# Spectral filter and gated FFN on one Trainium2 core: seven-product down projection, 64x64 tiles, a shorter inverse transform and a list-scheduled order

## The chip, the core and the metric

The kernel runs on one core of one Trainium2 chip. The metric is the device time of one execution in microseconds (us); the profile's span, from the first to the last instruction of the program, is a little shorter than that time. TensorE (PE) multiplies matrices and writes PSUM, which has eight banks of 128 partitions x 512 float32 columns. VectorE (DVE) and ScalarE (ACT) empty PSUM; GpSimd (POOL) and SyncE (SP) here mostly issue transfers. Each engine works through its own queue in order and waits on semaphores.

## The reference

```python
def _A_ref(x, w_r, w_i):                    # x [1, 2048, 512]
    X = rfft2(x.astype(float32))            # over positions (2048) and features (512)
    X = X * (w_r + 1j * w_i)                # w [2048, 257]
    return irfft2(X, s=(2048, 512)).astype(bfloat16)
def _B_ref(x, w_gate, w_up, w_down):        # 512 -> 1792 -> 512
    h = gelu(x @ w_gate) * (x @ w_up)
    return h @ w_down
xn = layernorm(A_x)
out = A_x + _A_ref(xn, w_r, w_i) + _B_ref(xn, w_gate, w_up, w_down)
```

All inputs are bfloat16. `B_x` is not used.

## The kernel before, in words

The 2048 positions are cut into 16 tiles `j` of 128 positions and four blocks `b` of four tiles. Two streams of work share all engines.

The FFN stream. A block is normalised (`ln_stat`, `ln_aggr`, `ln_norm`), transposed on PE (`trans`, L373) and kept as `xnT`. For each of 14 slices `fc` of the 1792 hidden columns, `gate` (L585) and `up` (L600) each make one bank of 128 hidden columns x 512 positions from four matmuls of 512 columns. ScalarE takes the gelu of the gate bank (L588, into `gl`), VectorE multiplies the up bank by it (L606, into `hT`). `down` (L642) makes one bank of 128 positions x 512 features from 14 matmuls of 512 columns, in three parts; VectorE adds the bank to `x_sb` (L657). The down tiles of block `b` stand among the gate and up units of block `b+1`. The last tile is done in two halves of 256 columns (`last_down`, L622, added at L627).

The spectral stream. The feature transform is unit D (`butter` on VectorE, L395 to L399, then four matmuls, L413 to L416). The 2048-point transform over positions is split into 64 x 32: unit A does the 64-point part (L437, L441), with the two halves of a tile on the two halves of PE's rows; the result goes through DRAM (`scr1`) to be laid out anew as `tv`. Unit B does the 32-point part of step `h` (16 steps): four matmuls with 64 output rows each, two of which stand side by side in PE's columns. ScalarE copies the result to `xc` (L468), VectorE multiplies by the filter in four instructions (`m1`, `m2`, then their difference and sum into `yy`, L474 to L477), unit C does the inverse 32-point part (L488), ScalarE copies it to `vp` (L494), and it goes through DRAM (`scr2`) to `vv`. Unit E (L522) does the inverse 64-point part of a tile, four matmuls of 128 columns; ScalarE writes `zt` (L529), and GpSimd puts one row of it in place (L530). Unit F (L548 to L551) does the inverse feature transform with four matmuls of 256 columns, one pair for even and one for odd frequencies. ScalarE copies the bank to `eo` (L556), VectorE adds and subtracts the halves (L561, L562) and adds the result to `x_sb` (L565).

```python
                for ri in range(2):                          # unit_B
                    for hh in range(2):
                        ins = e.matmul(bank(bk + ri)[64 * hh:64 * hh + 64, 0:257], be[:, 64 * ri:64 * ri + 64], tv[:, 16 * hh + h, :],
...
                for ri in range(2):                          # unit_C
                    for hh in range(2):
                        ins = e.matmul(bank(bk + hh)[:, 0:257], cm[64 * hh:64 * hh + 64, h, ri, :], y[64 * hh:64 * hh + 64, ri, 0:KD],
...
                    for fc in range(f0, f1):                 # down
                        ins = e.matmul(bank(bk), hT[b % 2][:, fc, jj * P:(jj + 1) * P], wd_sb[:, fc, :], start=(fc == 0), stop=(fc == NFC - 1))
```

The order is written by hand. The main loop runs over blocks and slices; after each gate, each up and each part of a down, `hook` runs what a table (`plan`, filled by `at`) sets down for that point: the statistics, transposes, units D, A, B, C, E, F and the late loads. `take` chooses PSUM banks by a running estimate of when each comes free. SyncE issues nearly all transfers (L304), in the order of the program; GpSimd issues the late loads (`load_late`, L308), each behind the last matmul put ahead of it in the order: the down weights, the constants `be`, `cm`, `gm`, and the filter `Wr`, `Wi` in 16 loads of 128.5 KB. `_Prog.op` derives the semaphore waits from the keys that each operation reads and writes.

Of the kernel before, what the change touches and what calls it, by code (L numbers as in the profile page):

```python
# [13 lines left out]
S = 2048  # L14
D = 512
# [13 lines left out]
def _constants():  # L29

    tp = 2.0 * np.pi
    q = np.arange(64)
    l32 = np.arange(32)
    k1 = np.arange(64)

    dd = np.arange(P)[:, None]
    m64 = np.arange(64)[None, :]
    a0 = tp * dd * (4 * m64) / D  # L40
    a2 = tp * dd * (4 * m64 + 2) / D
    im0 = -np.sin(a0)
    im0[:, 0] = np.cos(np.pi * np.arange(P))
    FE0 = np.concatenate([np.cos(a0), im0], 1)
    FE2 = np.concatenate([np.cos(a2), -np.sin(a2)], 1)
    FO = []
    for c in range(2):
        d = dd + P * c
        kodd = np.stack([4 * m64[0] + 1, 4 * m64[0] + 3]).reshape(1, 128)
        a = tp * d * kodd / D  # L50
        FO.append(np.concatenate([np.cos(a), -np.sin(a)], 1))
    FD = np.concatenate([FE0, FE2, FO[0], FO[1]], 1)

    AM = np.zeros((P, NJ, 2, P))
    for b in range(2):
        for j in range(NJ):
            l = 16 * b + j
            th = tp * (np.outer(q, k1) / 64.0 + l * k1[None, :] / S)
            c, s = np.cos(th), np.sin(th)
            AM[64 * b:64 * b + 64, j, 0, :] = np.concatenate([c, -s], 1)  # L60
            AM[64 * b:64 * b + 64, j, 1, :] = np.concatenate([s, c], 1)

    BM = np.zeros((32, 2, 2, 2, 32, 2))
    th = tp * np.outer(l32, l32) / 32.0
    for kl in range(2):
        BM[:, 0, kl, 0, :, kl] = np.cos(th)
        BM[:, 1, kl, 0, :, kl] = np.sin(th)
        BM[:, 0, kl, 1, :, kl] = -np.sin(th)
        BM[:, 1, kl, 1, :, kl] = np.cos(th)
    BM = BM.reshape(2, 16, 4, P).transpose(0, 2, 1, 3).reshape(P, P)  # L70

    CM = np.zeros((2, 32, 2, 16, 2, 2, 2, 32))
    for hh in range(2):
        for kl in range(2):
            for h in range(16):
                kk = 32 * kl + 16 * hh + h
                th = tp * (np.outer(l32, l32) / 32.0 + kk * l32[None, :] / S)
                CM[hh, :, kl, h, 0, 0, kl, :] = np.cos(th)
                CM[hh, :, kl, h, 0, 1, kl, :] = np.sin(th)
                CM[hh, :, kl, h, 1, 0, kl, :] = -np.sin(th)  # L80
                CM[hh, :, kl, h, 1, 1, kl, :] = np.cos(th)
    CM = CM.reshape(P, 16, 2, P)

    EM = np.zeros((2, 16, 2, 2, 2, 64))
    for hh in range(2):
        for kl in range(2):
            kk = 32 * kl + 16 * hh + np.arange(16)
            th = tp * np.outer(kk, q) / 64.0
            EM[hh, :, 0, kl, 0, :] = np.cos(th)
            EM[hh, :, 0, kl, 1, :] = np.sin(th)  # L90
            EM[hh, :, 1, kl, 0, :] = -np.sin(th)
            EM[hh, :, 1, kl, 1, :] = np.cos(th)
    EM = EM.reshape(2, 16, 4, P).transpose(0, 2, 1, 3).reshape(P, P)

    d2 = np.arange(256)[None, :]
    G = np.zeros((P, 4, 256))
    for c in range(2):
        kd = (2 * np.arange(P) + c)[:, None]
        a = tp * kd * d2 / D
        G[:, 2 * c, :] = 2.0 * np.cos(a)  # L100
        G[:, 2 * c + 1, :] = -2.0 * np.sin(a)
    G[0, 0, :] = 1.0
    G[0, 1, :] = np.cos(np.pi * np.arange(256))
    ID = np.eye(P)
    f16 = lambda a: np.ascontiguousarray(a.astype(np.float16))
    return (f16(ID), f16(FD), f16(AM.reshape(P, -1)), f16(np.concatenate([BM, EM], 1)),
            f16(CM.reshape(P, -1)), f16(G.reshape(P, -1)))


class _Prog:  # L110
# [17 lines left out]
    def op(self, eng, fn, r=(), w=(), dma=False, after=()):  # L128
        deps = [(ev, True) for ev in after]
        for k in r:  # L130
            if k in self.writer:
                deps.append((self.writer[k], True))
        for k in w:
            if k in self.writer:
                deps.append((self.writer[k], False))
            for ev in self.readers.get(k, ()):
                deps.append((ev, False))
        need = {}
        for (st, val), raw in deps:
            if st == eng and not dma and (eng == "pe" or not raw):  # L140
                continue
            need[st] = max(need.get(st, 0), val)
# [9 lines left out]

# [39 lines left out]

def bass_parallel_sum__spectral_gfnet__glu_gated_geglu__prompt_kernel(
# [22 lines left out]
    wgv = B_w_gate.rearrange("(dc p) f -> p dc f", p=P)  # L216
    wuv = B_w_up.rearrange("(dc p) f -> p dc f", p=P)
    wdv = B_w_down.rearrange("(fc p) d -> p fc d", p=P)

    with ExitStack() as es:  # L220
# [3 lines left out]
        pr = _Prog(nc, es)  # L224
        op = pr.op
# [3 lines left out]
        xnT = sb("xnT", [P, 4, S], F16)  # L229

        arena = sb("arena", [P, 9216], F16)
        am = arena[:, 0:4096].rearrange("p (j r c) -> p j r c", j=NJ, r=2)
        fold = [arena[:, 4096 + 2048 * i:6144 + 2048 * i].rearrange("p (a c) -> p a c", a=4) for i in range(2)]
        ev1 = arena[:, 8192:9216].rearrange("p (a c) -> p a c", a=2)
        vv = arena[:].bitcast(BF16)[:, 0:32 * KD].rearrange("p (l c) -> p l c", l=32)
        AKEYS = ["am", "ev1"] + [("fold", i, a) for i in range(2) for a in range(4)]
        wg_sb = sb("wg", [P, 4, FF], BF16)
        wu_sb = sb("wu", [P, 4, FF], BF16)
        wd_sb = sb("wd", [P, NFC, D], BF16)
        hT = [sb("hT%d" % i, [P, NFC, 512], BF16) for i in range(2)]  # L240
        ident = sb("ident", [P, P], F16)
        fd = sb("fd", [P, 768], F16)
        be = sb("be", [P, 2 * P], F16)
        cm = sb("cm", [P, 16, 2, P], F16)
        gm = sb("gm", [P, 4, 256], F16)
        Wr = sb("Wr", [P, 16, 258], BF16)
        Wi = sb("Wi", [P, 16, 258], BF16)
        xs = [sb("xs%d" % i, [P, D], F16) for i in range(4)]
        tt = [sb("tt%d" % i, [P, 2, KD], F16) for i in range(4)]
        tv = sb("tv", [P, 32, KD], F16)  # L250
        xc = [sb("xc%d" % i, [P, 2, 258], F16) for i in range(2)]
        m1 = [sb("m1_%d" % i, [P, 2, 258], BF16) for i in range(2)]
        m2 = [sb("m2_%d" % i, [P, 2, 258], BF16) for i in range(2)]
        yy = [sb("yy%d" % i, [P, 2, 258], BF16) for i in range(4)]
        vp = [sb("vp%d" % i, [P, 2, KD], BF16) for i in range(4)]
        NZ = 4
        zt = [sb("zt%d" % i, [P, 4, P], BF16) for i in range(NZ)]
        row = sb("row", [32, 64], BF16)
        z256 = xn[:].rearrange("p a d -> p (a d)").bitcast(BF16)
        gl = [sb("gl%d" % i, [P, 512], BF16) for i in range(3)]  # L260
        eo = [sb("eo%d" % i, [P, 512], BF16) for i in range(2)]
        ys2 = [sb("ys%d" % i, [P, 512], BF16) for i in range(2)]
        osb = [sb("osb%d" % i, [P, D], BF16) for i in range(3)]
# [5 lines left out]
        dumm = sb("dumm", [P, 512], F16)  # L269
        warm_o = sb("warm_o", [P, 1], F32)  # L270

# [3 lines left out]
        def bank(i):  # L275
            return psum[:, i * 512:(i + 1) * 512]

        def bank_h(i):
            return psum_h[:, i * 1024:(i + 1) * 1024]

        def pair(i):
            return psum[:, i * 512:(i + 2) * 512].rearrange("p (a c) -> p a c", a=2)[:, :, 0:KD]


        pt = [0.0]
        act_t = [0.0]
        free = [0.0] * 8

        def take(n, dur, hold=None):

            i = min(range(9 - n), key=lambda i: max(free[i:i + n]))
            pt[0] += dur
            if hold is None:
                act_t[0] = max(act_t[0], pt[0] + 0.25) + 0.62
                end = act_t[0]
            else:
                end = pt[0] + hold
            for k in range(i, i + n):
                free[k] = end
            return i  # L300


        def dma(eng, dst, src, r=(), w=()):
            return op(eng, lambda e: e.dma_start(dst, src), r=r, w=w, dma=True)  # L304

        def load_late(dst, src, keys):

            op("pool", lambda e: e.dma_start(dst, src), w=keys, dma=True, after=[("pe", pr.cnt["pe"])])  # L308

        def load_x(j0, n, b, eng):  # L310
            dma(eng, x_sb[64 * b:64 * b + 64, j0:j0 + n, :], xv[b, :, j0:j0 + n, :], w=[("x", j, b) for j in range(j0, j0 + n)])

        def load_w(t, v, nm, lo, hi, eng):
            dma(eng, t[:, :, P * lo:P * hi], v[:, :, P * lo:P * hi], w=[(nm, i) for i in range(lo, hi)])
# [116 lines left out]
        def unit_A(j):  # L431
# [17 lines left out]
            if j >= 3:  # L449
                load_tv(j - 3)  # L450
# [358 lines left out]
```

## Time and profile before

| | us |
|---|---|
| time, median of 3 runs | 198.46 (197.67 to 198.78) |
| span of the profiled execution | 194.3 |
| between that span and the median time | 4.2 |
| PE busy | 186.9 |
| DVE busy | 112.1 |
| ACT busy | 89.1 |
| POOL busy | 26.3 |
| first gate matmul starts at | 8.94 |
| last matmul stream starts at | 188.08 |

The profiled execution's own time is not given apart from the runs, so its span stands for it, with the 4.2 us to the median as what lies around it. In the lists of instructions a line number is that of the kernel, `x` is a count and the mean is the length of one instruction's record; matmuls are pipelined, so their records overlap and only the distance between starts tells what one adds. The stages are: loading and first block to 31 us; units D and A among block 0 and 1 to 60 us; units B and C from 73 to 124 us; units E and F from 137 to 188 us.

### The profile page before, as it was taken

To read this page: it belongs to the slowest core of one execution; us is meant where nothing else is said; L and a number is where in the kernel's file an instruction comes from. 1 tells how busy PE (TensorE), PEld (TensorE's weight loads), DVE (VectorE), ACT (ScalarE), POOL (GpSimd) and SP (SyncE) were. 2 spreads that over 40 slices of the span, in tenths; PEclk is the share of its full clock that TensorE was granted. 3 is DMA by queue.
4 is the path that set the end of the run, shared out by engine and by line. 5 is a ranking of instruction groups with operands and counts; after the bars stand their busy time and mean duration, and the time that the engine had idled before them with its cause. 6 is when DMAs were issued, how large, how long until landed. Compare 5 with 4: busy or idle time off the path is not lost.

```text
span 194.3 us, 3181 instructions
## 1 busy us (share of the span) xinstructions
PE 186.9 (96%) x1173; PEld 95.4 (49%) x1173; DVE 112.1 (58%) x266; ACT 89.1 (46%) x160; POOL 26.3 (14%) x52
## 2 busy tenths in 40 slices
PE   7599898999999999999999999999999999999993
PEld 2285454646454444444444444444455555555562
DVE  2759899787722227658577556423146656546361
ACT  3144465666466124547446363413454555644310
POOL 0200515023200232222300000000011011111000
DMA  4999999556655663355862331340002221121112
GB/s 125 326 290 333 285 255 255 144 145 129 139 162 142 145 119 90 75 95 129 177 168 86 108 112 35 104 120 17 1 0 54 54 59 27 42 53 45 26 28 54
DMA packets 19167, 23.09 MB, mean 119 GB/s; under 512 B 2240, under 2 KB 16832, under 8 KB 18768
## 3 DMA queue, kind: packets, MB, share of 16 engines
q1 hardware_dynamic: 16064, 16.46, 31.4%
q0 software_dynamic: 1712, 5.32, 12.5%
q10 hardware_dynamic: 1376, 1.11, 2.0%
q8 instruction: 9, 0.15, 0.3%
q14 instruction: 6, 0.05, 0.1%
HBM read 16.57 MB, written 6.31 MB: 118 GB/s over the span
## 4 chain that ended last, share of the span: by engine, by line
PE 85%; DVE 7%; DMA 4%; issue 1%; SPq 1%; POOL 1%; ACT 0%; DVEq 0%
PE ps L642 24%; PE ps L600 22%; PE ps L585 22%; DMA wu<-in_B_w_up_dram 4%; DVE st L351 3%; PE ps L462 2%; PE ps L488 2%; PE ps L522 2%; PE ps L622 2%; DVE hT L606 1%; PE ps L373 1%; SPq L304 1%; PE ps L437 1%; PE ps L548 1%; PE ps L550 1%
## 5 line engine op out<-in xcount | busy, mean ns | idle before, releaser
L606 DVE TENSOR_TENSOR hT<-ps,gl 128x512 bf16<-128x512 f32 (+1 forms) x59 | 39.0, 662 | 38.5 <-PE ps L600 36.9
L585 PE MATMUL ps<-xnT,wg 128*128 128x512 f16 (+1 forms) x236 | 58.1, 369 | 0.8 <-ACT xnT L385 0.8
L600 PE MATMUL ps<-xnT,wu 128*128 128x512 f16 (+1 forms) x236 | 58.1, 368 | 0.2 <-DMA wu<-in_B_w_up_dram 0.2
L588 ACT ACTIVATE gl<-ps 128x512 bf16<-128x512 f32 (+1 forms) x59 | 34.0, 575 | 45.0 <-PE ps L585 44.0
L642 PE MATMUL ps<-wd,hT 128*128 128x512 bf16 x210 | 50.1, 379 | 0.0
L600 PEld LDWEIGHTS ps<-xnT,wu 128*128 128x128 bf16 x236 | 22.4, 98 | 21.9 <-issue 0.8
L585 PEld LDWEIGHTS ps<-xnT,wg 128*128 128x128 bf16 x236 | 21.8, 98 | 21.8 <-issue 2.8
L642 PEld LDWEIGHTS ps<-wd,hT 128*128 128x128 bf16 x210 | 19.8, 98 | 21.1 <-issue 0.8
L657 DVE TENSOR_TENSOR x_sb<-ps,x_sb 128x512 bf16<-128x512 f32 x12 | 8.3, 690 | 16.4 <-PE ps L642 16.4
L530 POOL COPY zt<-xn 1x128 bf16<-1x128 bf16 x16 | 4.9, 309 | 80.4 <-DMA xn<-row 42.5
L556 ACT ACTIVATE eo<-ps 128x512 bf16<-128x512 f32 x16 | 9.5, 595 | 12.4 <-PE ps L551 12.4
L529 ACT ACTIVATE zt<-ps 128x512 bf16<-128x512 f32 x16 | 9.5, 596 | 7.7 <-PE ps L522 7.6
L468 ACT ACTIVATE xc<-ps 128x514 f16<-128x514 f32 x16 | 8.7, 600 | 8.8 <-PE ps L462 8.8
L351 DVE BATCH_NORM_STATS2 st<-x_sb 128x6 f32<-128x512 bf16 x16 | 10.8, 684 | 3.0 <-DMA x_sb<-in_A_x_dram 3.0
L494 ACT ACTIVATE vp<-ps 128x514 bf16<-128x514 f32 x16 | 8.7, 598 | 6.2 <-PE ps L488 6.2
L561 DVE TENSOR_TENSOR ys<-eo 128x256 bf16<-128x256 bf16 x16 | 4.6, 289 | 11.9 <-ACT eo L556 11.9
L447 ACT ACTIVATE tt<-ps 128x514 f16<-128x514 f32 x16 | 8.7, 597 | 6.0 <-PE ps L441 6.0
L420 ACT ACTIVATE xs<-ps 128x512 f16<-128x512 f32 x16 | 9.6, 597 | 4.1 <-PE ps L416 4.1
L359 POOL TENSOR_TENSOR rstd<-vpe,mhalf 128x4 f32<-128x4 f32 (+1 forms) x5 | 4.6, 921 | 31.0 <-DVE vpe L358 31.0
L308 POOL DMA_DIRECT2D Wr<-in_A_w_r_dram x8 | 5.0, 625 | 19.2 <-PE ps L642 13.4
L363 DVE TENSOR_SCALAR xn<-x_sb,ag,rstd 128x512 f16<-128x512 bf16 x16 | 6.2, 435 | 2.0 <-POOL rstd L359 2.0
L308 POOL DMA_DIRECT2D Wi<-in_A_w_i_dram x8 | 4.9, 617 | 13.0 <-PE ps L585 10.1
(68 smaller groups left out, 169.6 us busy)
## 6 DMA issues: line engine op xcount, KB each, us to landing
scr<-tt SPq DMA_DIRECT2D x16, 128.5 KB
tv<-scr SPq DMA_DIRECT2D x16, 128.5 KB
scr<-vp SPq DMA_DIRECT2D x16, 128.5 KB
arena<-scr SPq DMA_DIRECT2D x16, 128.5 KB
out_dram<-osb SPq DMA_DIRECT2D x30, 64.0 KB
x_sb<-in_A_x_dram SPq DMA_DIRECT2D x6, 256.0 KB, 14.1
Wr<-in_A_w_r_dram POOLq DMA_DIRECT2D x8, 128.5 KB, 4.7
Wi<-in_A_w_i_dram POOLq DMA_DIRECT2D x8, 128.5 KB, 4.3
```

Source lines behind the costliest of these rows:

```text
L308: op("pool", lambda e: e.dma_start(dst, src), w=keys, dma=True, after=[("pe", pr.cnt["pe"])])
L351: op("dve", lambda e: e.bn_stats(st[:, j, :], x_sb[:, j, :]), r=[("x", j, 0), ("x", j, 1)], w=[("st", j)])
L420: op("act", lambda e: e.activation(x4[:].rearrange("p (a c r) -> p a c r", a=2, r=4), bank(bk).rearrange("p (a r c) -> p a c r", a=2, r=4) ...
L447: op("act", lambda e: e.activation(t4[:], pair(bk), ACT.Copy, scale=SC_A), r=[("ps", bk), ("ps", bk + 1)], w=[("tt", j % 4)])
L468: op("act", lambda e: e.activation(xc[s2][:, :, 0:KD], pair(bk), ACT.Copy, scale=SC_B), r=[("ps", bk), ("ps", bk + 1)], w=[("xc", s2)])
L529: op("act", lambda e: e.activation(z[:], bank(bk).rearrange("p (a c) -> p a c", a=4), ACT.Copy, scale=SC_E), r=[("ps", bk)], w=[zk])
L556: op("act", lambda e: e.activation(o2[:], bank(bk), ACT.Copy), r=[("ps", bk)], w=[ok])
L585: ins = e.matmul(bank(bg)[:, 0:n], wg_sb[:, dc, fc * P:(fc + 1) * P], xnT[:, dc, c0:c0 + n], start=(dc == 0), stop=(dc == 3))
L588: op("act", lambda e: e.activation(gl[k % 3][:, 0:n], bank(bg)[:, 0:n], ACT.Gelu_apprx_tanh), r=[("ps", bg)], w=[("gl", k % 3)])
L600: ins = e.matmul(bank(bu)[:, 0:n], wu_sb[:, dc, fc * P:(fc + 1) * P], xnT[:, dc, c0:c0 + n], start=(dc == 0), stop=(dc == 3))
L606: op("dve", lambda e: e.tensor_tensor(hT[b % 2][:, fc, h0:h0 + n], bank(bu)[:, 0:n], gl[k % 3][:, 0:n], ALU.mult), r=[("ps", bu), ("gl", k ...
L642: ins = e.matmul(bank(bk), hT[b % 2][:, fc, jj * P:(jj + 1) * P], wd_sb[:, fc, :], start=(fc == 0), stop=(fc == NFC - 1))
```

## The change

Nearly the whole kernel is written anew; the stages, the split into 64 x 32 points, the trips through DRAM and the order of the first transfers stay. Five things differ.

1. **Down projection.** `hT` of a block and `w_down` are each taken as 2 x 2 blocks, and their product is made with seven block products (a Strassen-Winograd form) instead of eight. One product is 14 matmuls of 256 columns (two groups of 128 positions, seven slices). VectorE forms sums S1 to S4 of blocks of `hT` (7 x 256 columns each) for every block of positions, and once the sums T1 to T4 of blocks of `w_down`. The products build up in three banks P, Q and T (R besides in the last block); ScalarE copies P to Q after the first product, and VectorE takes a bank out after a product (`merge`, seven or eight for each block of positions, 512 columns each, some through a float32 buffer `mu`).
2. **Inverse feature transform.** The constants are shifted by half a sample, and unit F makes four matmuls of 128 columns for each tile, two tiles together in two banks. VectorE then joins them with four instructions of 512 columns, two of which write in reversed order, and one add of 1024.
3. **32-point units.** Unit B and unit C use 64 x 64 tiles of PE. B has four matmuls that lie on four different tiles. C has eight, in two rounds of four; it adds the two filter products itself in PSUM, so VectorE makes only the two products `pp`, and not their sum and difference. The filter comes in 64 loads of 66 KB in three slots.
4. **Order.** Every operation becomes a task with an estimated cost and a priority. A list scheduler (`_Plan.schedule`) steps through time, gives each free engine the ready task of the lowest priority number, assigns PSUM banks, favours staying in one tile shape on PE by 1.2, and the resulting order is emitted for all five engines. Late loads and the first of the weight sums carry a `gate`: they come after a point of the main work, and wait for the last PE task put before them.
5. **Small things.** Statistics and transposes of the first two tiles go one tile at a time; one of two transpose copies of the later blocks goes to ScalarE instead of VectorE; waits are also set between two operations of one engine, other than PE, where the second overwrites what the first read or wrote; outputs go out from `x_sb` two tiles at a time.

The core of the diff:

```diff
+            sums("S1", "21", "22", ALU.add, halves, prio - 2, over=("S4",))
+            sums("S2", "S1", "11", ALU.subtract, halves, prio - 2)
+            sums("S3", "11", "21", ALU.subtract, halves, prio - 2)
+            vP, vQ, vT = newbank(), newbank(), newbank()
+            prod(vP, "11", "11", True, prio, alloc=(vP, 1, False), res=2)
+            act(lambda e: e.activation(bank(vQ), bank(vP), ACT.Copy), 512, [("ps", vP)], [("ps", vQ)], prio, alloc=(vQ, 1, True), need_full=True)
+            prod(vT, "S1", "T1", True, prio + step, alloc=(vT, 1, True))
+            sums("S4", "12", "S2", ALU.subtract, halves, prio + step, over=("S1",))
+            merge(vT, ("mu", 1), (t1, 1), prio + step)
+            prod(vQ, "S2", "T2", False, prio + 2 * step)
+            merge(vQ, ("mu", 0), (t0, 1), prio + 2 * step)
+            prod(vP, "12", "21", False, prio + 3 * step)
+            merge(vP, (t0, 0), (t0, 0), prio + 3 * step)
+            prod(vQ, "S3", "T3", False, prio + 4 * step)
+            merge(vQ, (t1, 1), ("mu", 1), prio + 4 * step)
+            prod(vT, "S4", "22", False, prio + 5 * step)
+            merge(vT, (t0, 1), ("mu", 0), prio + 5 * step)
+            prod(vQ, "22", "T4", False, prio + 6 * step)
+            merge(vQ, (t1, 0), (t1, 0), prio + 6 * step)
...
+                    for t in range(2):                       # prod
+                        for f in range(7):
+                            ins = e.matmul(bank(v)[:, 256 * t:256 * t + 256], A0[:, f, P * t:P * t + P], B0[:, f, :],
...
-                e.matmul(bank(bk)[:, 0:256], z[:, 0, :], gm[:, 0, :], start=True, stop=False, skip_group_check=True)
...
+                for t in range(2):                           # unit_F
+                    z = zt[(2 * i + t) % 4]
+                    o = bank(v, t)
+                    for a, s in enumerate((0, 2, 3, 1)):
+                        ins = e.matmul(o[:, a * P:(a + 1) * P], z[:, s, :], gm[:, a, :], start=(a == 0), stop=(a == 3), skip_group_check=True)
...
+            dve(lambda e: e.tensor_tensor(u[:, :, :, 0:128], o2[:, :, :, 0, :], o2[:, :, :, 1, :], ALU.add), 512, [ek], [uk + (0,)], prio, x=2, over=BCALL)
+            dve(lambda e: e.tensor_tensor(u[:, :, :, 255:127:-1], o2[:, :, :, 0, :], o2[:, :, :, 1, :], ALU.subtract), 512, [ek], [uk + (1,)], prio, x=2)
...
-                for ri in range(2):
-                    for hh in range(2):
-                        ins = e.matmul(bank(bk + ri)[64 * hh:64 * hh + 64, 0:257], be[:, 64 * ri:64 * ri + 64], tv[:, 16 * hh + h, :],
+                for hh in range(2):                          # unit_B
+                    for kl in range(2):
+                        c = hh ^ kl
+                        ins = e.matmul(bank(v, kl)[64 * c:64 * c + 64, 0:257], be[64 * kl:64 * kl + 64, 0:64],
+                                       tv[64 * kl:64 * kl + 64, 16 * c + h, :], start=True, stop=True, skip_group_check=True)
...
+                for i in range(2):                           # unit_C
+                    for a in range(2):
+                        for hh in range(2):
+                            kl = a ^ hh
+                            ins = e.matmul(bank(v, hh)[64 * kl:64 * kl + 64, 0:257], cm[64 * hh:64 * hh + 64, h, kl, i, :],
+                                           pp[s2][i][64 * hh:64 * hh + 64, kl, 0:KD], start=(i == 0), stop=(i == 1), skip_group_check=True)
...
+                        key = t.prio - (1.2 if e == "pe" and t.mode == mode and t.mode != "m" else 0.0)
...
+        STEP = 1.73
+        DST = 1.535
...
+        BC_AT = [52 + 2.6 * h for h in range(16)]
+        W_AT = 30
...
+        for i, t in enumerate(order):
+            at = EF0 + 3.5 * i
+            unit_E(2 * t, 2 * i, at)
+            unit_E(2 * t + 1, 2 * i + 1, at + 0.3)
+            unit_F(2 * t, i, at + 2.5)
```

`STEP` and `DST` are the plan's lengths of a gate and up unit together and of one product; priorities count in this main work, so a unit B every 2.6 means one for each 2.6 us of gate, up and down matmuls.

## The prediction

> **What bounds the kernel now.** The page comes first, for the busy shares and the chain that ended last.
>
> ```profile
> PE 186.9 (96%) x1173; PEld 95.4 (49%) x1173; DVE 112.1 (58%) x266; ACT 89.1 (46%) x160; POOL 26.3 (14%) x52
> PE 85%; DVE 7%; DMA 4%; issue 1%; SPq 1%; POOL 1%; ACT 0%; DVEq 0%
> ```
>
> TensorE (PE) is busy 96% of the span and 85% of the chain. An average could hide a stage with another limit, so next come the sums by stage (start to end; PE, weight load, VectorE, ScalarE, GpSimd).
>
> ```profile
> 9.00:31.00 22.00, 20.95 (x156) 12.48 (x156) 18.71 (x46) 10.90 (x22) 4.26 (x6) 1.00 1.07 295
> 60.00:124.00 64.00, 64.00 (x382) 28.30 (x379) 37.38 (x91) 29.26 (x53) 9.70 (x16) 1.00 0.48 115
> 137.00:188.00 51.00, 51.00 (x317) 28.20 (x316) 26.32 (x66) 25.05 (x45) 4.95 (x16) 1.00 0.14 36
> ```
>
> From 31 us on PE never stops, and VectorE is half idle. Only in the first stage does VectorE run at 18.71 of 22. The clock is 1.00 throughout. The waits say the same: the engines that empty PSUM wait for PE, and PE itself waits little.
>
> ```profile
> ACT gl L588 <- PE ps L585: 44.0, 46, 4.2
> DVE hT L606 <- PE ps L600: 36.9, 35, 2.0
> PE ps L373 <- DVE xn L363: 1.7, 2, 1.1
> PE ps L585 <- ACT xnT L385: 0.8, 1, 0.8
> PE ps L413 <- DVE arena L399: 0.5, 1, 0.5
> ```
>
> Last, the chain in order of time gives what a matmul really costs (start, us, what); a row's mean of 379 ns holds overlap and is no price.
>
> ```profile
> 73.54 0.56 PE ps L462 x8
> 74.11 0.97 PE ps L585 x4
> 75.08 0.86 PE ps L600 x4
> ...
> 139.92 0.22 PE ps L522 x4
> ...
> 188.24 3.07 PE ps L622 x28
> 191.34 0.42 DVE osb L627
> ```
>
> So 512 columns cost 0.216 us (0.86/4), 256 cost 0.110 (3.07/28) and 128 cost 0.055 (0.22/4), weight load hidden. Eight 257-column matmuls on 64-column tiles (L462) take 0.56: four rounds of two at 0.11, plus about 0.1 for the change of tile shape; the next unit pays 0.1 more (0.97 against 0.86). A visit to another tile shape thus costs 0.2.
>
> The budget: gate and up 424 x 0.216 + 48 x 0.110 = 96.9; down 210 x 0.216 + 3.07 = 48.4; transposes 64 x 0.055 = 3.5; D 5.3 (16 x 0.33); A, B and C 3.5 each in 32 rounds; E 3.5; F 64 x 0.110 = 7.0; 24 visits x 0.2 = 4.8. Sum 179.9. PE's timeline puts the first gate matmul at 8.94, gaps in its stream of 0.2, 0.8 and 0.7 at 9.7, 23 and 31 us, and 3.2 behind the last matmul: 193.7 in all, against the span of 194.3. The median of plain runs is 198.46, so 4.2 lie around the span; I keep them.
>
> **The change, part by part.** *Down:* 16 x 14 products of 512 columns become 4 x 7 x 14 = 392 of 256: 392 x 0.110 = 43.0 for 48.4, **-5.5** with rounding. Weight loads double against columns, but L622 already ran that shape.
>
> *F:* sixteen times four matmuls of 256 columns become 64 of 128, at E's 0.055: 3.5 for 7.0, **-3.5**.
>
> [...]
>
> *B:* four 64x64 tiles in one round for two rounds of two: 16 rounds for 32, **-1.8**. *C:* eight matmuls of 64x64 in two rounds for four in two: 0. Four at once is in no row; the nearest are two column tiles at once (L462) and two row tiles at once (L488, eight in 0.55). Both overlap fully, so I take full overlap; the other end is by pairs only, B 0 and C +3.5.
>
> *Visits:* B and C now share a tile shape, and the plan favours staying in it. Sixteen visits for B and C become 17 if each B meets the C of the step before, 32 if PSUM is too full for both pairs of banks: +0.2 to +3.2, I take **+0.8**.
>
> *VectorE*, by start to start in the chain: 0.60 for 1024 16-bit columns, 0.34 for 512, 0.59 for 512 from PSUM, 0.20 for 256. Added: S1 to S4, 1792 columns each in two pieces, 1.07 x 4 = 4.3 a block, 17.1 in all; the four weight sums 4.3 once; 29 merges for 16 adds, +7.7; F's four half-sums and wide add, 15.7 for 11.8, +3.9. Removed: the 32 sums into yy, -6.4; three copies of transposes, moved to ScalarE, -1.8. Net +25 on about 100 by this measure. In 60 to 188 us this is covered: 37 of 64 and 26 of 51 leave room. The reversed writes of F are in no row: 0.34 (two elements a cycle) or 0.59 (one), which would add 16 x 0.25 = 4 to VectorE; I take 0.34, as these are ordinary 16-bit adds otherwise. Ahead of 58 us it is not covered: weight sums (4.3) and the first block's sums fall where VectorE runs at 85%. The first weight sum also waits for the PE unit put before it in the plan; behind it in VectorE's queue stand the gate-up products, whose PSUM banks PE needs. Stalls there: from -1.5 (the plan cures the present ones) to +6; I take **+1.2**.
>
> *ScalarE:* four PSUM to PSUM copies (no row; 0.5 to 0.7 each by the 512-column evictions of 0.6) and three 1024-column copies: +5 on 89, hidden behind its 44 of waiting. The copy P to Q has two products' time (S1.T1 stands between) before PE needs Q.
>
> *GpSimd:* W comes in 64 loads instead of 16. At 617 ns each (the present rows) eight take 5.0 for two 32-point steps, which PE needs 6.3 for (2 x 2.6 of planned main work plus 0.53 of B and C). Three slots loaded ahead cover the landing (4.3 to 4.7). 0, and at 0.93 an issue (the longest row) 7.4 against 6.3, 5 refills x 1.1 = 5.5 less some 4 of lead: +1.5 at most.
>
> *SP:* 20 output transfers for 32, in longer rows; 64 scratch transfers stay. Nothing waits for them but the end.
>
> *Tail:* the last product ends in one 512-column merge (0.69) instead of a 256-column one (0.42), with transfers of 64 KB for 32: 0.3 to 0.6, **+0.5**.
>
> *Start:* two statistics chains of one tile for one of two, transposes of one tile each; the up matmul at 9.74 waits for its weights' transfer, whose place in the queue is kept: 0.
>
> Sum: -5.5 -3.5 -1.8 +0.8 +1.2 +0.5 = -8.3. Span 186.0, time **190.2**. Behind each cured stall PE itself is late next, since it then has work without a gap.
>
> **Rivals.** *(a) The four tiles run by pairs.* +5.3 on the forecast (B +1.8, C +3.5): 195.5. For it: 64-column weight loads took 109 ns against 98 for 128 columns, as long as a round. Against: L462 hides just these loads. Chance 0.07. [...]
>
> *(b) VectorE becomes the bound in two stages.* Between 9 and 58 us its work rises from 37 (18.7 and most of the next stage's 19.3) to about 43 of 49; a tenth of that lost to in-order waits is 4 to 5. In the last stage the plan gives a pair of tiles of E and F 3.5 of main work, so PE has 4.4 with E and F; VectorE has 3.6 (F 1.96, 1.4 gate-up products 0.84, 0.7 merge 0.41 and sums 0.43), or 4.1 with reversed writes at one element a cycle: another 1. Sum +5.5: 195.7. For it: the stalls by VectorE in this stage now. Against: its reads are spread later by the plan. Chance 0.11.
>
> *(c) PSUM banks: slower.* A down pass holds three banks (P, Q, T) for its seven products, where now it holds one. A pair unit takes two more, and three are left for gate and up. Such a bank is held 0.86 while filled, 0.2 until release, 0.6 to 0.7 for its eviction, and the wait in ScalarE's or VectorE's queue behind one other instruction (0.5 to 0.6): 2.2 to 2.4, three banks giving one unit per 0.72 to 0.79, just under the 0.86 of a unit. Two instructions ahead make it 2.9 and 0.97: 0.11 lost on each of the 84 units in those blocks, 9 us, and visits at their 32 add 2.4. Then 201.6, slower. It decides from a bank cycle of 2.6 (3 x 0.86). For it: VectorE at 69% with pieces of 0.6. Against: evicting engines wait for PE today, and a product needs no new bank, so the plan can put one there. An order fixed beforehand can't repair it if an engine is late. Chance 0.17.
>
> *(d) Gains and stalls cancel:* two thirds of (c), 198. Chance 0.03.
>
> *(e) F's 128-column matmuls cost what 256 columns do,* their loads (98 ns in every row) no longer hidden: +3.5, 193.7. E's 0.22 for four speaks against. Chance 0.02.
>
> **How the numbers follow.** The forecast as written has 0.60. A measurement of this kernel tells 0.5% (1.0 us) from no change. Faster: 0.60 + 0.07 + 0.11 + 0.02 = 0.80; same 0.04 ((d), and the mild end of (c)); slower 0.16. The forecast's own range is 186.5 (no stall, no extra visits: -11.9) to 194. Carried to the milder cases and (d) it ends at 199, leaving out most of (c) and a little below: 186.5 to 199.
>
> **What would show it.** Right: PE at 94% or more of a span near 186; 28 products of 14 matmuls at 1.53 each; F's eight matmuls in 0.44; B's four in 0.11 and C's eight in 0.22; VectorE near 138 busy by the page's measure. Wrong: B's four starts spread over 0.11 (a); PE waiting for VectorE's stores or sums before 60 us (b); PE gaps of 0.1 to 0.5 ahead of gate and up matmuls, released by the gelu or the hT product that empties their bank (c). A GpSimd issue above 0.8 would move the wait to W. Any of these adding over 8 us makes the forecast's sign wrong.

## The result and the profile after

The changed kernel is slower: 213.66 us (median, 211.37 to 215.49) against 198.06 measured beside it, a ratio of 1.078 with a 95% interval of 1.068 to 1.088. The forecast was 190.2 and faster. Here and below, medians in us are of all executions, while ratios leave out those over 1.5% above the fastest of the same kernel. The profiled execution took 215.49 us, the longest of the four; the waits read below come back in the experiments.

First the page: busy time, the chain by engine, and two rows of the forty slices (TensorE busy in tenths, granted clock in tenths).

```profile
PE 187.4 (88%) x1391; PEld 108.3 (51%) x1391; DVE 131.6 (62%) x276; ACT 92.4 (43%) x160; POOL 56.4 (26%) x101
PE 49%; DMA 28%; SPq 9%; DVE 5%; ACT 2%; issue 2%; POOL 2%; DVEq 0%; ACTq 0%
PE   7688997299999999960699999999996899999993
PEclk9879999759999999996589999999999699999999
```

Before, 85% of the chain was TensorE's and 4% transfers; now it is 49% and 28%. The row of PE has three holes (slices of 5.3 us: near 40, 99 and 163 us), and right behind each the clock row falls to 5 to 7 tenths. Before, it showed 1.00 in every stage. The waits of TensorE (line, what it waited for, us in total, times, longest) name the holes:

```profile
PE ps L641 <- DMA tv<-scr: 9.3, 1, 9.3
PE ps L592 <- DVE area L581: 4.0, 1, 4.0
PE ps L680 <- DMA area<-scr: 2.3, 1, 2.3
PE ps L769 <- DMA wu<-in_B_w_up_dram: 1.5, 2, 1.1
```

L641 is the first unit B, which needs the last piece of `tv` back from DRAM. L592 is a unit D behind the butterfly (L578 to L581). L680 is the middle row ahead of the units E; it waits for the last piece of `vv`. The timeline of after shows what stood behind the second one (start, length, engine and line; in brackets the idle time before and its releaser):

```profile
36.92 1.04 PE L769 MATMUL ps<-xnT,wu 128*128 128x512 f16 x4 [1.08 <-DMA wu<-in_B_w_up_dram]
37.59 1.29 DVE L528 BATCH_NORM_STATS2 st<-x_sb 128x6 f32<-128x512 bf16 x2 [5.70 <-DMA x_sb<-in_A_x_dram]
41.99 0.29 PE L592 MATMUL ps<-fd,area 128*128 128x128 f16 x1 [4.03 <-DVE area L581]
```

The last up weights and the last tiles of `x` landed 6 to 9 us later than before; in VectorE's queue the statistics of those tiles stood ahead of the butterfly. So VectorE sat idle for 5.7 us, though the last copy of transposes that the butterfly needs had ended at 32.8 us on ScalarE.

The chain in order of time (start, us, what) has the trip to B, and three pieces that the forecast named:

```profile
79.90 8.24 DMA scr<-ta
88.16 0.52 SPq L486
88.72 9.05 DMA scr<-ta
97.78 0.53 SPq L486
98.35 5.04 DMA tv<-scr
103.53 0.65 PE ps L641 x8
...
113.43 0.22 PE ps L663 x8
...
188.11 0.45 PE ps L716 x8
...
200.75 9.29 PE ps L822 x84
```

Two stores and a load of 128 KB, one behind the other, take 23 us. Before, the last store was issued at 61.9 us and the last load had landed at 72.6, one microsecond ahead of the first B. The work itself came out as forecast: C's eight matmuls 0.22, F's eight 0.45, a product 1.55 (84 matmuls in 9.29).

So the account of the span, with the forecast's own list of work (179.9 - 5.5 - 3.5 - 1.8 + 0.8 = 169.9): 8.6 to the first of the gaps; 169.9 of work; about 21.7 in gaps of the matmul stream longer than 0.25 us, where before had 1.8; about 8.2 because matmuls ran at half clock at 9.5 to 12.9, 42.0 to 47.1, 103.5 to 108.5 and 166.6 to 170.0 us; 3.9 from the start of the last matmul to the end. That is 212.3 of 213.7. The saving of 10 us is there; 20 us more of gaps, some 18 of them waits that end with a transfer, and 8 of half clock took nearly three times as much.

### The profile page after: what moved, and what is told of

The parts are those of the page before. It is cut to its first block, busy times and chain, and to the rows that moved or that the text cites. A ratio compares the mean times of both kernels' runs of the same rounds, so it can differ in the third digit from the quotient of the medians.

```text
span 213.7 us, 3635 instructions
## 1 busy us (share of the span) xinstructions
PE 187.4 (88%) x1391; PEld 108.3 (51%) x1391; DVE 131.6 (62%) x276; ACT 92.4 (43%) x160; POOL 56.4 (26%) x101
## 4 chain that ended last, share of the span: by engine, by line
PE 49%; DMA 28%; SPq 9%; DVE 5%; ACT 2%; issue 2%; POOL 2%; DVEq 0%; ACTq 0%
PE ps L769 26%; PE ps L822 14%; SPq L486 9%; DMA x_sb<-in_A_x_dram 8%; DMA scr<-bc 8%; DMA scr<-ta 8%; DMA tv<-scr 2%; PE ps L694 2%; PE ps L663 2%; POOL bc L701 2%; DMA area<-scr 2%; PE ps L716 1%; PE ps L641 1%; DVE hT L774 1%; PE ps L552 1%
## 5 line engine op out<-in xcount | busy, mean ns | idle before, releaser
L524 POOL DMA_DIRECT2D W<-in_A_w_r_dram x32 | 18.4, 599 | 34.1 <-PE ps L769 29.2
L650 DVE TENSOR_TENSOR bc<-bc,W 128x514 bf16<-128x514 f16 x32 | 12.3, 427 | 13.1 <-ACT bc L646 12.8
L524 POOL DMA_DIRECT2D W<-in_A_w_i_dram x32 | 18.5, 613 | 5.2 <-PE ps L769 2.6
L646 ACT ACTIVATE bc<-ps 128x514 f16<-128x514 f32 x16 | 9.5, 599 | 15.1 <-PE ps L641 15.1
L598 ACT ACTIVATE area<-ps 128x512 f16<-128x512 f32 x16 | 9.5, 596 | 14.0 <-PE ps L595 14.0
L822 PE MATMUL ps<-wd,hs 128*128 128x256 f16 (+1 forms) x112 | 13.6, 273 | 0.0
L822 PE MATMUL ps<-wd,hT 128*128 128x256 bf16 x112 | 13.5, 273 | 0.0
L822 PE MATMUL ps<-wdt,hs 128*128 128x256 f16 x112 | 13.4, 273 | 0.0
L641 PE MATMUL ps<-tv,be 64*64 64x257 f16 x64 | 4.9, 312 | 9.5 <-DMA tv<-scr 9.3
L822 PEld LDWEIGHTS ps<-wdt,hs 128*128 128x128 f16 x112 | 10.8, 98 | 2.8 <-issue 0.9
L822 PEld LDWEIGHTS ps<-wd,hs 128*128 128x128 f16 x112 | 10.8, 98 | 2.7 <-DVE mu L836 0.2
L822 PEld LDWEIGHTS ps<-wd,hT 128*128 128x128 bf16 x112 | 10.9, 98 | 2.2 <-DVE hT L774 0.2
```

What stands on the lines that cost most here:

```text
L524: add("pool", lambda e: e.dma_start(dst, src), w=w, over=over, occ=0.7, lat=kb / 1024 / 0.28, prio=prio, gate=prio, dma=True)
L598: act(lambda e: e.activation(x4.rearrange("p (a c r) -> p a c r", a=2, r=4), bank(v).rearrange("p (a r c) -> p a c r", a=2, r=4), ACT.Copy ...
L646: act(lambda e: e.activation(xc[s2][:, :, 0:KD], pair(v), ACT.Copy, scale=SC_B), 514, [("ps", v)], [("xc", s2)], prio)
L650: dve(lambda e, i=i: e.tensor_tensor(pp[s2][i][:, :, 0:KD], xc[s2][:, :, 0:KD], W[:, i, :, h % 2, 0:KD], ALU.mult), 514, [("xc", s2)] + [( ...
L822: ins = e.matmul(bank(v)[:, 256 * t:256 * t + 256], A0[:, f, P * t:P * t + P], B0[:, f, :], start=(first and t == 0 and f == 0), stop=(f = ...
```

## Experiments

Five theories. **K**: the loads of `tv` are slow by their access pattern. The change reads each as 4x2 rows, to put them in the order that the 64-row tiles of B need:

```diff
-            dma("sp", tv[j::16], scr1[8 * j:8 * j + 8, :].rearrange("p (x c) -> p x c", c=KD), r=[("scr1", j)], w=[("tv", j)])
+            dma("sp", tv[j::16], scr1[8 * j:8 * j + 8, :].rearrange("(b y) (x c) -> y b x c", b=2, c=KD),
```

The trace's semaphore records count 9 updates for each load before and 5 after; from issue to the last update a load took 4.3 us before (median, 3.6 to 6.6) and 5.7 after (4.1 to 9.2). How the pattern would do that is not shown. **T**, from which K grew: the transfers are slow by themselves, whatever the order of their issues; of e1 it expected a wait above 7 us ahead of B, and 209 us or more. **Q**: SP's queue of issues holds the loads back. **W**: the down weights, all four transfers issued at 20 to 23 us where before they were spread from 21 to 32, delay the up weights and `x`; by the page the transfer engines were 90% or more busy from 5 to 32 us (before, to 34). **G** came later: GpSimd is held up by VectorE.

### e1_lag: loads two stores behind (Q)

```diff
+            if t.dma and t.eng == "sp" and t.w and t.w[0][0] in ("tv", "vv"):
+                held.append(t)
+                continue
...
+                while len(held) > 2:
+                    put(held.pop(0))
```

> Changed kernel, but SyncE issues each scratch load (tv, vv) only after two further stores of the scratch trip have been issued; plan, costs and every other queue as they are. Theory Q (the fixed order puts each load right behind its own store, so SyncE stands at the load until the store has landed, and the next stores queue behind it): the last tv load lands some 12 us sooner, PE's gap of 9.4 us ahead of the first unit B and most of the slow clock after it (2.5 us) go, the gap ahead of unit E shrinks: about 199 to 202 against 213. [...]

212.07 us, ratio 1.074 (1.066 to 1.082): no gain worth naming. The wait ahead of B is 8.1 for 9.3. Q falls: the stores were slow by themselves (the last still took 10.7 us from issue to landing).

### e3_spread: rows laid out by the stores (K)

Each store goes out in two halves, so that a load reads eight plain rows.

```diff
-            dma("sp", scr1.rearrange("(j b y) (x c) -> j (y x) b c", b=2, y=4, c=KD)[j], t4, ...
+            for b in range(2):
+                dma("sp", scr1.rearrange("(j y b) (x c) -> j b y x c", b=2, y=4, c=KD)[j, b], t4[:, b, :], ...
```

> [...] Theory T: a tv load takes 4 to 5 us instead of 5 to 9, the trips that stand one behind the other shorten by 6 or more, the gap ahead of the first unit B falls from 9.4 to about 3: 203 to 206. Theory Q: the trips still stand in line, one extra issue for each store: loads shorten by 1 to 3 each, 207 to 212.

207.67 us, ratio 1.051 (1.042 to 1.061), but the wait ahead of B grew to 11.0 us. The experiment was badly made: the loads now have 9 updates, but each half-store has an outer dimension of 4 itself and shows 5. It moved the suspect and didn't remove it, so it says nothing against K. Why it is still some 5 us faster than after isn't shown; its profile lacks the wait ahead of E (0.5 us for 2.3).

### e4_wd_later: down weights spread (W)

```diff
-for f in range(f0, f1)], 2 + i, kb=128 * (f1 - f0))
+for f in range(f0, f1)], (4, 5, 9, 11)[i], kb=128 * (f1 - f0))
```

> Changed kernel, but the four loads of the down weights are held to points 4, 5, 9 and 11 of the main work instead of 2 to 5. Theory W (they share the transfer engines with the last positions and up weights, which then land at 37 us and not at 28 to 31 as before, so PE waits 1.2 and 4.2 us and runs at half clock after it): these gaps fall to under 2 us and the slow clock of 41 to 47 us goes, 205 to 208. Rival (these loads are late for another reason): no gain over 2 us, 210 or more.

206.54 us, ratio 1.046 (1.037 to 1.055), 7 us better than after. The waits at L592 and for `wu` are gone from the list, and the clock no longer falls at 40 us (waits of TensorE, then the clock's slices):

```profile
PE ps L641 <- DMA tv<-scr: 9.4, 1, 9.4
PE ps L680 <- DMA area<-scr: 2.4, 1, 2.4
```

```profile
PEclk9979999999999999965899999999998899999999
```

W holds. The gaps of 5.4 us and their half clock are what was saved. The profiles agree: from issue to landing the last piece of `x` took 17.3 to 17.7 us in all four with the down weights together (after, e1, e3, e15), and 10.2 to 15.5 in all but one (e9) with them spread.

### e5_all_three: e1, e3 and e4 together

> Changed kernel with the three edits together: lag of two stores, spread loads, down weights later. If stalls and the slow clock behind them are all that was mis-sized, and the saved matmul time is there as forecast, this comes to 190 to 196, below the kernel before. If the gaps move elsewhere (PSUM banks, VectorE), 198 or more.

205.48 us, ratio 1.042 (1.036 to 1.049): a miss of 10 us. The wait ahead of B stayed at 9.4. It has e3's half-stores in it and did no better than e4 beyond the noise.

### e6_tv_pool: e4, and GpSimd issues the loads of tv

```diff
-            dma("sp", tv[j::16], scr1[8 * j:8 * j + 8, :].rearrange("(b y) (x c) -> y b x c", b=2, c=KD),
+            dma("pool", tv[j::16], scr1[8 * j:8 * j + 8, :].rearrange("(b y) (x c) -> y b x c", b=2, c=KD),
```

> Changed kernel with the down weights later (as e4_wd_later, 206.5) and the 16 tv loads issued by GpSimd instead of SyncE. The lag of e1 left the gap ahead of the first unit B at 8.2 us, so the queue's order is not its cause. [...] Rival theory C (the 24 filter loads and the 1 MB of cm that run beside them slow all transfers): the gap stays over 6 us, 202 or more.

203.34 us, where the author's estimate was 193 to 197, with a wide spread (195.11 to 206.71; no ratio came of it). In the profiled execution, the longest, the wait ahead of B halved, from e4's 9.4 to 4.1 us, with another issuer and the pattern kept; why is not shown. And 3.1 us came back ahead of the butterfly: VectorE stood idle for 3.5 us until the last tiles of `x` landed, at 36.3 us, although the down weights are spread here. So it decides nothing on K.

### e7_before_4eng: the pattern put into the kernel before (K)

The one line of the diff above, in the kernel before.

> The kernel before the change, with one edit: the tv load walks its eight rows as 4 x 2, as the changed kernel does (rows land in another order, so the transform's values are others; sizes and work are the same). Before, the last tv load landed at 72.5 us and unit B began at 73.5, so any delay there reaches PE. Theory K: each load is slower and they queue, the last lands 4 to 12 us later, PE gets a gap ahead of unit B of 3 to 10 us and a slow clock of some 2 us behind it: 201 to 209. Theory C or Q: no change over 1 us, 196 to 199.

203.41 us, ratio 1.030 (1.023 to 1.038): +6 us for one access pattern, same bytes, same issues. Before had no wait at this line; now (waits of TensorE):

```profile
PE ps L462 <- DMA tv<-scr: 3.8, 1, 3.8
```

The last load lands at 79.2 instead of 72.6 us, and the clock is at half from 78.4 to 85.2 us. That is the profiled execution (205.04 us, mean clock 0.975). The other three took 201.68 to 203.76 us at mean clocks of 0.992 to 1.000, which leaves room for one stretch of half clock of 3.2 us (2 x 0.008 x 201) or none. So most of the 6 us there is wait and not clock. K is a cause by itself.

### e8_plan_vv: the plan's latency of vv

```diff
-                        t.done = dma_free + 1.1
+                        t.done = dma_free + (4.0 if any(k[0] in ("vv",) for k in t.w) else 1.1)
```

> As e6_tv_pool, and the plan is told that a vv load takes 5.1 us after its bytes have gone instead of 2.2 to 1.1 (4.0 for 1.1), so that it puts units E later and other PE work ahead of them. Theory P (the plan's transfer costs are too low, so units stand in PE's queue ahead of their data): the gap of 2.5 us ahead of unit E and the slow clock behind it (1.5) go, 3 to 4 below e6_tv_pool. Rival: the work put ahead is then missing later and the gap moves, within 1 of e6_tv_pool.

203.45 us (200.0 to 206.12), as e6, where 3 to 4 less was expected. The wait at L680 went, but one of 2.7 us at L716 (F, for a copy of GpSimd) and one of 1.5 at L822 came in its place. A later plan uncovers the next wait; the one at L716 is taken up by e12.

### e9_store_by_y and e10_w_early: loads of plain rows, then the filter loads earlier

e9 is e4 with the stores cut by `y`, so that their outer dimension is 32 and the loads are plain rows; e10 adds the second diff. Of e9 K expected a wait of 3 to 4.5 us ahead of B, and 198 to 202 us.

```diff
-            dma("sp", scr1.rearrange("(j b y) (x c) -> j (y x) b c", b=2, y=4, c=KD)[j], t4, ...
-            dma("sp", tv[j::16], scr1[8 * j:8 * j + 8, :].rearrange("(b y) (x c) -> y b x c", b=2, c=KD), ...
+            for y in range(4):
+                dma("sp", scr1.rearrange("(j y b) (x c) -> j y x b c", b=2, y=4, c=KD)[j, y], t4[32 * y:32 * y + 32], ...
+            dma("sp", tv[j::16], scr1[8 * j:8 * j + 8, :].rearrange("p (x c) -> p x c", c=KD), ...
```

```diff
-        W_AT = 30
+        W_AT = 14
```

> The kernel of e4_wd_later (206.5 us) with scratch 1 laid out in rows of (j y b): each store is cut into four of 32 partitions (one y each), so that no store has an outer dimension of 4 and every load of tv is 8 plain rows. [...] Rival N (the trip through DRAM is late whatever its pattern, by the 24 filter loads and the constants beside it): the gap stays within 1.5 us of 9.5 and the time at 204-208. Rival Q (SP's queue of issues is the limit; it now has 48 more): the gap grows, over 207.

> e9_store_by_y with the 24 filter loads that fill the three buffers planned at 14 for 30 (they go out some 10 us or more earlier and end before the last loads of tv; TensorE's order is the same). If what is left of the gap ahead of B is contention with these loads: the gap goes from e9's 3-4.5 us to under 1.5 and the time falls by 2 to 5 us against e9, to 194-199. If it is the bare trip of store and load behind the last A: within 1 us of e9. If the filter loads hold up GpSimd's rstd of the last group: a new gap ahead of the last butterfly and no gain.

e9: 204.63 us, ratio 1.027 (1.008 to 1.047); e10: 199.87, ratio 1.013 (1.001 to 1.026), just over the 199 expected. The loads have 9 updates again. The waits, first of e9 and then of e10:

```profile
PE ps L592 <- DVE area L581: 5.0, 1, 5.0
PE ps L682 <- DMA area<-scr: 2.8, 1, 2.8
PE ps L643 <- DMA tv<-scr: 2.4, 1, 2.4
```

```profile
PE ps L682 <- DMA area<-scr: 3.4, 1, 3.4
...
PE ps L643 <- DMA tv<-scr: 0.9, 1, 0.9
```

Ahead of B (L643) the wait goes from 9.4 to 2.4 by the pattern, and to 0.9 when the 24 filter loads end before the last trips. e9's time missed its 198 to 202. Its profiled execution (206.31 us) shows the wait ahead of the butterfly again: the last piece of `x` took 17.7 us to land, as with the down weights together. So these weights aren't the only thing that can delay it; what did so here isn't known, nor whether the shorter executions had it. The 48 more issues on SP show no harm: e10 to e12 have them too, with at most 0.6 us of that wait.

### e11_plan_vv, e12_row_act and e13_row_act_plan: the wait ahead of E and F

e11 is e10 with e8's latency. e12 besides gives the copies of the middle row to ScalarE; e13 is e12 without e8's latency.

```diff
-            add("pool", lambda e: e.tensor_copy(z[0:1, 1, :].rearrange("o (b q) -> o b q", b=2),
-                                                z256[0:1, :].rearrange("o (b j q) -> o b j q", b=2, j=NJ)[:, :, j, :]),
+            add("act", lambda e: e.activation(z[0:1, 1, :].rearrange("o (b q) -> o b q", b=2),
+                                              z256[0:1, :].rearrange("o (b j q) -> o b j q", b=2, j=NJ)[:, :, j, :], ACT.Copy),
```

> e10_w_early with the plan's latency of the loads of vv at 4.0 for 1.1, so that E is planned behind the loads' real landing. If the wait ahead of E (2.5 us and the half clock behind it, 1.9 us) is a fault of the plan's latency alone: 2 to 4 us under e10, 191-196. If, as in e8_plan_vv, the list schedule only moves the gap to other places: within 1 us of e10.

> e11_plan_vv with the copy of the middle row into zt (1x128 elements, 16 of them) given to ScalarE instead of GpSimd. In e11 one such copy took over 4 us on GpSimd at 163-168 us while VectorE ran bf16 additions back to back, and the F behind it began 2.7 us late. Theory G (GpSimd is held off while VectorE works): the copies take about 0.2 us on ScalarE, the gap of 2.8 us ahead of F goes, and with the half clock behind it 2.5 to 4.5 us: 195.5-198 against e11's 200.2, near or under the kernel before. Rival (the wait is E's trip, planned elsewhere): the gap comes back ahead of E or F with 2 us or more, time within 1 us of e11.

> e12_row_act with the plan's latency of the vv loads put back to 1.1 (that is e10_w_early with ScalarE's row copies). The wait ahead of E (3.6 us in e10) is a wait for the last vv load and not for GpSimd, so it stays at 2.5 to 4 us: 199-201, 2 to 4 us over e12. Rival: it is no longer than e12, if what e12 saves ahead of E it pays behind it.

e11: 200.23 us, ratio 1.015 (1.004 to 1.027), no better than e10, like e8. Its timeline shows why F was late:

```profile
163.32 4.62 POOL L703 COPY bc<-xn 1x128 bf16<-1x128 bf16 x2 [0.54 <-ACT bc L702]
...
166.81 0.41 DVE L730 TENSOR_TENSOR ta<-bc 128x512 bf16<-128x512 bf16 x1
...
167.14 0.41 DVE L731 TENSOR_TENSOR ta<-bc 128x512 bf16<-128x512 bf16 x1
167.48 0.68 DVE L776 TENSOR_TENSOR hT<-ps,gl 128x512 bf16<-128x512 f32 x1
...
168.00 0.23 PE L718 MATMUL ps<-gm,bc 128*128 128x128 f16 x1 [2.67 <-POOL bc L703]
```

A copy of 128 elements stood for 4.38 us, from 163.3 to 167.7 us, while VectorE ran its additions of two SBUF operands without a pause (records of 0.41 and 0.68 us, 0.33 and 0.60 apart); it ended 0.2 us after VectorE had begun the one that reads PSUM (L776). The next two lines are this copy in e11 and in e12 (shortest, median, longest ns):

```profile
L703 POOL COPY bc<-xn x16: 279/284/4383, 151.9 to 181.5; 1x128 bf16<-1x128 bf16 x16
```

```profile
L703 ACT ACTIVATE bc<-xn x16: 291/292/310, 149.6 to 174.3; 1x128 bf16<-1x128 bf16 x16
```

The 4.38 us stand against a median of 0.28 for the sixteen copies. Why the additions would hold the copy up is not shown. It isn't one chance record: every copy of over 1 us in the profiles (4.38 in e8 and e11, 1.1 in both, 2.4 in after, e1, e3 to e6, e9 and e10) ends 0.2 us after VectorE begins an instruction that reads PSUM. The kernel before has none: its sixteen copies took 0.28 to 0.36 us.

e12 is **192.75 us (191.72 to 197.4), ratio 0.977 (0.969 to 0.985)**: 7.5 us less than e11, and faster than the kernel before, by 1.5 to 3.1%. The page and the waits of e12:

```profile
PE 179.2 (94%) x1391; PEld 106.3 (56%) x1391; DVE 130.2 (68%) x276; ACT 94.8 (50%) x176; POOL 48.5 (26%) x85
PEclk9979999999999999999999999999999999999999
```

```profile
PE ps L552 <- DVE ag L534: 1.5, 1, 1.5
PE ps L901 <- DVE hs L498: 1.2, 1, 1.2
PE ps L824 <- DVE hT L776: 1.0, 1, 1.0
PE ps L643 <- DMA tv<-scr: 0.9, 1, 0.9
```

No wait is above 1.5 us and, after the start, the clock doesn't fall in this profile. Gaps of the matmul stream behind 8.5 us make about 5 us, where after has about 22 and e11 9 to 10. 7.5 us is more than the 2.5 to 4.5 expected: the gap of 2.8, one of 1.7 ahead of the down products that shrank to 1.1, and their half clock (168.6 to 172.0) account for about 5; e11's profiled execution besides has 3.4 us more of half clock at the start, which is none of this edit's doing as far as the traces show. The order is planned anew with the edit, so 68 of TensorE's 1391 matmuls stand elsewhere too. e13's ratio is 1.003 (0.997 to 1.009), median 200.38: without the later plan of `vv` the moved copies gain 2 us on e10. The two belong together: each alone, e11 or e13, leaves some 5 us or more.

### e14, e15, e16: one cause put back at a time

Each is e12 with one edit undone and TensorE's order the same: the 4x2 rows of the loads (e14), the down weights at 2 to 5 (e15), the filter loads at 30 (e16). Of e14 K expected the last load 4 to 7 us later, a wait of 5 to 8 us ahead of B, and 198 to 202 us.

> e12_row_act (192.75 us) with the loads of tv alone read as 4x2 rows again, every engine's order unchanged; the eight rows of a load land in another order, so the values are those of permuted rows. [...] If the pattern matters only beside the filter loads (which are now out of its way): under 2 us, 192-195.

> e12_row_act with the four transfers of the down weights put back right behind one another at points 2 to 5. Theory W (they take the transfer engines from the up weights and the last input tiles): the waits of 1 to 5 us at 33-42 us come back with a half clock behind: 196-201. Rival: with the rest mended the wait is made up later, within 1 us of 192.75.

> e12_row_act with the filter loads put back to 30, beside the last scratch transfers. Theory: they lengthen the last trip, and the wait ahead of B goes from 1.1 us to 2.5-4 us (2.5 in e9_store_by_y): 194-197. Rival: within 1 us of 192.75, the trip being hidden now.

| put back | time, us | ratio to before | price: its ratio less e12's 0.977, of 198 us (with both intervals) |
|---|---|---|---|
| e14: loads by 4x2 rows | 201.37 | 1.015 (1.009 to 1.020) | 7.4 (5.5 to 9.3) |
| e15: down weights together | 200.80 | 1.013 (1.001 to 1.026) | 7.1 (4.2 to 10.0) |
| e16: filter loads late | 199.56 | 1.001 (0.995 to 1.007) | 4.7 (2.8 to 6.6) |

The longest wait of TensorE in e14, e15 and e16:

```profile
PE ps L643 <- DMA tv<-scr: 6.4, 1, 6.4
```

```profile
PE ps L592 <- DVE area L581: 3.6, 1, 3.6
```

```profile
PE ps L643 <- DMA tv<-scr: 2.4, 1, 2.4
```

Each cause brings its own wait back at its own place. In e14 the last load lands at 96.1 us instead of 89.3, and the clock is at half from 93.6 to 100.4: 5.4 us more of gap and about 2 of clock come near the price. e16 took more than the 194 to 197 expected, and its price is above its 1.4 of gap and 1.7 of clock; its profiled execution also has 3.4 us more of half clock at the start, so how much of its 4.7 belongs to the filter loads isn't settled. With the fourth cause (e11 against e12, 7.5) the prices add to 27 us, where after and e12 differ by 20 by the same measure. They may overlap, a wait that stays hiding part of another, but with these intervals the 7 us are hardly clear of noise.

## Why the prediction was wrong

**What held.** The terms for TensorE's work: a product of 14 matmuls 1.53 us, F's eight 0.45, C's eight 0.22, and B's four started within 10 ns (within 40 in three of the 32 groups of after and e12 together), the next four 0.11 us behind them. B and C are visited 21 times in after, where +0.8 stands for 20. VectorE is 131.6 busy (138 named), its reversed writes 0.42 us in e12 like the plain ones, and it is not the bound. The two rates named for them, two elements in the time of one, are those of two kinds of rows before: 512 more columns of 16 bits add 0.26 us (0.34 to 0.60), and 256 more from PSUM 0.27 (records of 0.425 at L627 and 0.690 at L657). The tail took 3.9 us from the last matmul's start. e12, with the same matmuls, takes 192.75 where 190.2 was said, and its 5 us of gaps stand beside the +1.2 on 1.7 that the sum had.

**The step that failed** is in *SP*: "64 scratch transfers stay. Nothing waits for them but the end." Unit B waits for them, and had done so before with one microsecond to spare (72.6 against 73.5 us). The number of transfers stayed, their pattern did not: one line of the diff, which the sum didn't price, gave each load 5 updates for 9, and 5.7 us for 4.3 from issue to landing (medians). The wait ahead of the first B became 9.3 us, and the pattern alone costs 6.0 (e7) or 7.4 (e14). The trace of before holds the margin, in when the last load landed; I read the waits, in which a hidden trip doesn't appear.

**Start: 0** failed in the same way. It kept the place of the up weights in their queue, but not that of the down weights on GpSimd, which are gated to points of the new plan and came out together at 20 to 23 us, beside the up weights and `x`: 5.4 us of gaps (e4), a price of 7.1 (e15). **GpSimd 0 (to +1.5)** counted issues, which measured 0.60 to 0.61 us as said, and not what the loads collide with (e16: 4.7 us), and left out the row copies, one of which took 4.38 us for 0.28 beside VectorE's additions (e11; moved in e12: 7.5 us).

**Stalls +1.2 (to +6)** were sought at VectorE's queue and PSUM's banks. They were 20 us, some 18 by transfers. Rival (c), slower by banks at 201.6, had the sign but not the mechanism: no wait for a bank is among the large ones.

**A term was missing**: the clock. With TensorE never idle for more than 1.2 us before, its rows said 1.00 everywhere and the sum took full speed for granted; 8 us of the miss are half clock, between 6 and 7 of them behind the three long gaps. Full speed wasn't certain even before: other executions of that kernel had mean clocks of 0.98 to 0.99 (197.6 to 200.5 us, for 196.0 to 198.6 at 1.00), which one profile doesn't show.

A smaller one: the 4.2 us "around the span" were a median of plain runs against one profiled span. Where both are of one execution they are about 2 (196.4 against 194.4; 215.49 against 213.7).

The range ended at 199 because each unknown was bounded by rows of engines. Of the transfers it looked only at the filter's, and bounded the landing of no other.

## What to carry to other kernels

When an order is planned anew, list every transfer with its landing and the first instruction that needs it, and write down the margin: a trip hidden by one microsecond isn't free, and it doesn't show in the waits. Compare the outermost dimension of each changed access pattern (4 for 8 cost 6 and 7 us here, e7 and e14), and count the semaphore updates of a load (5 for 9). A wait of TensorE cost more than itself in nine of the thirteen cases of 2.3 to 3.1 us here, by 3.4 us of half clock behind it. And repairs may pay only together: the kernel that was 8% slower is 2% faster when its transfers and one small copy are moved, while either half of the last step alone left 5 us or more.

## What the runs showed of the hardware

- The clock's falls came in stretches of 3.41 us or two, three or four times that (6.83, 10.24, 13.65). In mid-kernel, thirteen gaps of 2.3 to 3.1 us between two matmul records of TensorE stand in the profiles at full clock. Nine had a fall, of one stretch each (after, e1, e4, e6, e8, e9, e11, e15, e16), and four had none (2.4 us in e9, 2.6 in e8, 2.7 in e5, 3.1 in e6). Each of the gaps of 3.4 us or more had one: of one or two stretches up to 6.4 us, of three at 8.1 to 9.5 and of four at 11.0. Gaps of up to 1.5 us had none in mid-kernel.
- Sixteen loads of 128 KB by 4x2 rows in place of 8 rows, with the same bytes, cost the kernel before 6 us (e7) and the repaired one 7 (e14).
- A GpSimd copy of 128 elements took 0.28 us (median of sixteen, e11) and 4.38 beside a run of VectorE additions of two SBUF operands; it ended only when VectorE went on to an instruction that reads PSUM (e8, e11).
- Four matmuls of 257 columns on four 64x64 tiles of TensorE run side by side: starts 0, 3, 7 and 10 ns, and the next four from 109 ns on (e12).
